# Half of batch 6's first product as seven half products a pair, u added by accumulating DMA in batches 5 and 6, and two tail units moved behind batch 6

## The chip, the cores and the metric

The kernel runs on one core of one Trainium2 chip. The metric is the device time of one execution in microseconds, lower is better. The core has five engines that run their own instruction streams in order and meet through semaphores: TensorE (PE in the profile, its weight loads PEld), VectorE (DVE), ScalarE (ACT), GpSimd (POOL) and SyncE (SP). DMA transfers are issued from the queues of SP, GpSimd and ScalarE.

## The reference

Eight batches of 576 tokens go through a linear attention with eight heads of 64, and then through a mixer with a low-rank product over the tokens and a two-layer product over the channels:

```
q_p, k_p = [relu(q)*cos, relu(q)*sin], [relu(k)*cos, relu(k)*sin]   # cos, sin of the position
kv = k_p^T v ;  z = sum of k_p over the tokens                      # per batch and head
x  = (q_p kv) / (q_p z + 1e-6)                                      # 576 x 512 per batch
u  = x + V^T (U^T x)                                                # rank 32, over the tokens
out = u + relu(u @ w_ch1) @ w_ch2                                   # 512 -> 2048 -> 512
```

Inputs and output are float32; the kernel computes the products in bf16.

## The kernel before, in words

**Tiling.** The 576 tokens of a batch are held as four chunks of 128 and a tail of 64. The tails of two batches share one tile of 128 rows, so there are four tail pairs (`pr`), the last of batches 6 and 7. `u_bf[b]` holds u of a batch, `uT[b]` its transpose, made by DMA transposes on SP's queue (`utr_dma`), two chunks each. `uT_tl[pr]` is the transpose of a tail pair.

**First product.** `g1_main(b, j)` computes one block of 128 of the 2048 hidden rows for 512 tokens: four 128x512 matmuls into a PSUM bank, then a relu on ScalarE into `hid[b]`. There are 16 blocks per batch. `g1_tail(pr, jq)` does four blocks for a tail pair with sixteen 128x128 matmuls.

In batch 7 the first product is done by Strassen-Winograd instead. Blocks p and p + 8 are a *pair*; rows, tokens and the inner dimension are each cut in two, and seven products of half size take the place of eight. `g1_cross(b, p, i)` is one of the seven (two 128x256 matmuls) and `g1_join(b, p, ...)` brings them together: P1, U2 and P5 are copies of PSUM into `kept` by ScalarE, C11, C12 and C22 additions by VectorE, with relus on both. The steps of a pair are named `opened` (products 1 and 2, P1, C11), `second` (6 and 5, U2, P5), `third` (7, C22) and `closed` (3 and 4, C12, relus, `max`). The products 3 to 7 need sums of weights (`w1_sum`, four, each in two halves of columns; half 1 serves pairs 4 to 7) and sums of quarters of u transposed (`uT_sum`, four a batch), which VectorE makes beforehand.

**Second product.** Batches 2 to 7 do it by the same scheme in `half_part(b, n, k, form)`: fourteen half parts of eight 128x256 matmuls a batch. It needs sums of `hid` (`hid_sum`, VectorE). The results go to float32 tiles `o_sb` (eight buffers), onto which u is added. In most batches VectorE adds u as it reads PSUM. In batches 5 and 6 (`LENT`) ScalarE copies PSUM, and GpSimd adds u in `half_store` with a 128x512 `tensor_tensor`, just before the store. Batch 5's stores go through GpSimd's queue, batch 6's through SP's.

**Order.** All is ordered by hand. `slots` is a list of units of TensorE work; `put(at, f)` hangs f behind slot number `at`. A unit's instructions and what hangs behind it go into each engine's stream in that order. In the slots of batch b's first product, half parts of batch b - 1 alternate with blocks of batch b: batch 5 starts at slot 156 and batch 6 at slot 190, with four tail units of pair 2 (slots 186 to 189) between them, batch 7 at slot 220. Behind the slots hangs the attention of a later batch (`attention_plan`): `q_prep`, `k_prep`, `v_prep`, the DMA transposes of q, `kv_unit`, five `x_unit`s, `A_unit` (U^T x), `u_mm` (V^T times that), four `u_add`s (VectorE, u = x + that) with the transposes of u between them, and `u_tail` for the tails of two batches. Its place is a number `w` per batch in `PLAN`; batch 7's is 191, so that its first `x_unit` stands at slot 195, the last at 203, `A_unit` at 205, `u_mm` at 207 and its last transposes of u at 212.

**PSUM.** There are eight banks: g0, g1, g2, T, o0, o1 and X, which is a pair of banks. In batches 3 to 6 blocks of the first product alternate between g0 and g1, half parts use o0 and o1, `x_unit` uses X. `A_unit` uses g2 (called "s"). `u_mm` and `u_tail` want four banks, one for each quarter of the rank-32 product: X's two, T and g2. A bank is free for its next use when the last reader of its content is done.

Of the kernel before, what the change touches and what calls it, by code (L numbers as in the profile page):

```python
# [17 lines left out]
def kernel(  # L18
# [446 lines left out]

    va = {}

    def u_mm(b, *spare):
        if b not in u_bf:
            u_bf[b] = pool.tile([P, 4, 4, P], BF16, tag="u_bf", bufs=3, name="u_bf")  # L470
        va[b] = four_banks(*spare)
        for c in range(4):
            for j in range(4):
# [11 lines left out]
            in1=va[b][j].rearrange("p (c n) -> p c n", c=4), op=ALU.add,  # L485
        )

    def u_tail(pr, *spare):
        u_tl[pr] = pool.tile(
            [P, DM], BF16, tag="k_p" if pr == 3 else "u_tl", bufs=1, name="u_tl"  # L490
        )
        vt = four_banks(*spare)
        for i in range(2):
            for j in range(4):
# [6 lines left out]
        for j in range(4):  # L501
# [8 lines left out]

    def uTt_alloc(pr):
        if pr not in uT_tl:
            uT_tl[pr] = pool.tile([P, 4, P], BF16, tag="uT_tl", bufs=1, name="uT_tl")

    def utr_dma(b, c0, c1):
        if c0 < 4:
# [113 lines left out]

    def uT_sum(b, i):

        if i == 1:
            t = pool.tile([P, 4, 2, 2, P], BF16, tag="vst", bufs=1, name="uT_s")
            for n in range(4):
                uT_s[b, n + 1] = t[:, n]
# [10 lines left out]
    def g1_cross(b, p, i):  # L647

        if (b, p) not in cross:
            if b not in hid:
                hid[b] = pool.tile([P, NJ, 512], BF16, tag="hid", bufs=2, name="hid")
            xy, z = [
                psum.tile([P, 512], FP32, tag=tag, bufs=1, name="c_ps") for tag in CROSS[p % 2]
            ]
            cross[b, p] = {"X": xy[:, 0:256], "Y": xy[:, 256:512], "Z": z[:, 0:256]}
        w = cross[b, p]
        cs = slice(p * P, p * P + P)
        to, lhs, rhs, first = {  # L660
            1: lambda: ("X", W1[0], uT_quarter(b, 0, 0), True),
            2: lambda: ("Y", W1[1], uT_quarter(b, 1, 0), False),
            3: lambda: ("Z", w1_s[4], uT_quarter(b, 1, 1), False),
            4: lambda: ("X", W1[3], uT_s[b, 4], False),
            5: lambda: ("Z", w1_s[1], uT_s[b, 1], True),
            6: lambda: ("X", w1_s[2], uT_s[b, 2], False),
            7: lambda: ("X", w1_s[3], uT_s[b, 3], False),
        }[i]()
        for d in range(2):
            nc.tensor.matmul(  # L670
                out=w[to].rearrange("p (c t) -> p c t", c=2), lhsT=lhs[:, d, cs],
                rhs=rhs[:, d], start=(first and d == 0), stop=(d == 1),
                skip_group_check=not first,
            )

    def g1_join(b, p, i):

        w, lo, hi = cross[b, p], slice(0, 256), slice(256, 512)
        top, low = hid[b][:, p, :], hid[b][:, p + 8, :]

        def relu(o, x):
            nc.scalar.activation(out=o, in_=x, func=AF.Relu, bias=0.0, scale=1.0)

        if i == "C11":
            diff(top[:, lo], w["P1"], w["Y"], ALU.add)
        elif i == "C22":
            diff(low[:, hi], w["P5"], w["X"], ALU.add)
            relu(low[:, hi], low[:, hi])
        elif i == "C12":
            diff(top[:, hi], w["U2"], w["Z"], ALU.add)  # L690
            relu(low[:, lo], w["X"])
            V_.tensor_scalar(out=top, in0=top, scalar1=0.0, scalar2=None, op0=ALU.max)
        else:
            if (b, "kept") not in cross:
                cross[b, "kept"] = pool.tile([P, 2, 3, 256], FP32, tag="q_pT", bufs=1, name="kept")
# [239 lines left out]
    def half_store(b, n, i):  # L935
        eng = nc.gpsimd if b < B - 2 else nc.sync
        c = n + 2 * i
        if b in LENT:
            o = halves[b, n]["o"][i]
            add(G_, by_n(o), by_n(o), u_bf[b][:, :, c, :])  # L940
        eng.dma_start(  # L941
            out=out[b].rearrange("(m k) n -> m k n", k=9)[:, c : c + 6 : 5, :],
            in_=halves[b, n]["o"][i],
        )
# [28 lines left out]
    def spare(at):  # L973
# [11 lines left out]
        4: (100, (-20, 1, V_, V_), (-13, 2, A_, V_), -12, (-9, -4, -4)),  # L985
        5: (127, (-24, 2, A_, A_), (-14, 2, A_, V_), (-14, -8, -5), (-8, -4, -4)),
        6: (157, (-23, 2, A_, A_), (-14, 2, A_, V_), (-14, -8, -6), (-8, -4, -4)),
        7: (191, (-24, 2, A_, A_), (-14, 2, A_, V_), (-14, -12, -10), ()),
    }

    def attention_plan(b):
# [42 lines left out]
        put(a_at, A_unit, tag=True)  # L1034
        odd = b % 2 == 1


        def two(at):
            return [T1, ("s", 1)] if at >= 88 else [spare(at)] * 2

        plan.append((w + a_at + 2, lambda: u_mm(b, *two(w + a_at + 2))))
        for j in range(4):
            put(a_at + 2 + j + (2 if b > 4 and j > 1 else 0), u_add, j)
        put(a_at + 3, utr_dma, 0, 2)
        put(a_at + (7 if b > 4 else 5), utr_dma, 2, 4)
        if odd:
            plan.append(
                (w + a_at + 9, lambda: u_tail(b // 2, *two(w + a_at + 9)))
            )
# [307 lines left out]
    for b in range(3, B - 1):  # L1357
# [10 lines left out]
        if b % 2:  # L1368
            tail_slots(b // 2)
        if b == 3:  # L1370
            tail_out(b // 2)

    at = len(slots)
# [7 lines left out]
    sums(b7 - 1, 0, (at, at + 1, at + 6))  # L1381
    sums(b7 - 1, 1, (at + 13, at + 15, at + 19))

    def opened(p):
        g1_cross(b7, p, 1)
        g1_cross(b7, p, 2)
        g1_join(b7, p, "P1")
        g1_join(b7, p, "C11")

    def second(p):  # L1390
        g1_cross(b7, p, 6)
        g1_cross(b7, p, 5)
        g1_join(b7, p, "U2")
        g1_join(b7, p, "P5")

    def third(p):
        g1_cross(b7, p, 7)
        g1_join(b7, p, "C22")

    def closed(p):  # L1400
        g1_cross(b7, p, 3)
        g1_cross(b7, p, 4)
        g1_join(b7, p, "C12")

    def group(p, first, then):
        def go():
            if p < 8:
                first(p)
            if p > 0:
                then(p - 1)  # L1410

        return go

    groups = [
        group(p, *fs) for p in range(9) for fs in ((opened, third), (second, closed))
    ]
    halfs = [(n, i7) for n in range(2) for i7 in range(7)]
# [8 lines left out]
    for i, go in enumerate(groups):  # L1426
        slots.append(go)
        if i < 14:
            n, i7 = halfs[i]
            slots.append(lambda n=n, i7=i7: half_part(b7 - 1, n, i7, "with g"))  # L1430
            if i7 > 4:
                put(len(slots), lambda n=n, i7=i7: half_store(b7 - 1, n, i7 - 5))
        else:
            slots.append(lambda j=i - 14: tail_cross(j))
    at = len(slots)
# [76 lines left out]
```

## Time and profile before

| | us |
|---|---|
| median of 3 runs | 295.01 (293.94 to 295.38) |
| the profiled execution | 294.26 |
| its span | 292.5 |
| mean granted clock of TensorE | 0.998 |

Stretches of the span and what the engines were busy in them (us):

| stretch | length | PE | DVE | ACT | POOL |
|---|---|---|---|---|---|
| 176.35 to 206.69: first product of batch 5, second of 4 | 30.34 | 30.08 | 20.68 | 19.24 | 5.44 |
| 206.69 to 210.41: four tail units of pair 2 | 3.72 | 3.72 | 3.58 | 2.89 | 0.62 |
| 210.41 to 225.90: batch 6, first half | 15.49 | 15.33 | 8.70 | 7.30 | 1.09 |
| 225.90 to 240.19: batch 6, second half | 14.29 | 14.19 | 10.87 | 6.11 | 4.45 |
| 240.19 to 269.95: first product of batch 7, second of 6 | 29.76 | 29.04 | 21.69 | 17.88 | 6.71 |
| 269.95 to 292.50: second product of 7 and the last tails | 22.55 | 18.50 | 13.77 | 3.67 | 5.21 |

How to read it: an engine whose busy time fills a stretch sets its length, and the others wait for it. Busy time alone does not show waits inside a stretch; for these the timeline gives each instruction with its start, its duration and, in brackets, the idle time before it and what ended that. "L576" is line 576 of the kernel. Names are those of the program: `g_ps` is PSUM of a whole block, `c_ps` of a half product of the first product, `h_ps` of a half part, `x_ps`, `a_ps`, `va_ps` of `x_unit`, `A_unit` and `u_mm` or `u_tail`, `gt_ps` of a tail unit.

### The profile page before, as it was taken

How to read it: one execution, taken by the hardware profiler on the slowest of the kernel's cores; microseconds unless marked ns; L12 is line 12 of the kernel's file. 1: busy time of each engine (PE TensorE's matmuls, PEld its weight loads, DVE VectorE, ACT ScalarE, POOL GpSimd, SP SyncE). 2: the span in 40 equal slices, each digit the busy share in tenths (PEclk: the TensorE clock that was granted, in tenths of full speed). 3: DMA queues.
4: the chain of work that ended last, by engine and by line, in shares of the span. 5: the costliest groups of instructions: out<-in, count | busy, mean ns of one | idle time of the engine just before them, and what ended most of it. 6: DMA issues, size and time to landing. Idle time of an engine off the chain costs nothing.

```text
span 292.5 us, 7212 instructions
## 1 busy us (share of the span) xinstructions
PE 284.3 (97%) x2884; PEld 191.8 (66%) x2920; DVE 203.6 (70%) x484; ACT 166.9 (57%) x340; POOL 55.8 (19%) x92
## 2 busy tenths in 40 slices
PE   8999999999999999999999999999999999999994
PEld 4675564447545446676767667766776667889883
DVE  5977855496875697556547793778827687865773
ACT  2955742276882767577736765298753445567210
POOL 6520500000020004202300501040202331302330
PEclk9999999999999999999999999999999999999999
DMA  7999999999998989998799939974800321101023
GB/s 226 304 254 251 275 160 222 205 318 228 340 194 175 294 212 259 240 315 237 147 250 265 242 88 280 231 266 92 215 0 4 110 68 59 50 24 72 2 94 125
DMA packets 90949, 54.07 MB, mean 185 GB/s; under 512 B 58564, under 2 KB 87620, under 8 KB 90916
## 3 DMA queue, kind: packets, MB, share of 16 engines
q1 hardware_dynamic: 84420, 43.94, 60.2%
q0 software_dynamic: 6304, 9.47, 14.6%
q8 instruction: 23, 0.38, 0.5%
q10 hardware_dynamic: 192, 0.20, 0.2%
q14 instruction: 10, 0.08, 0.1%
HBM read 36.86 MB, written 9.44 MB: 158 GB/s over the span
## 4 chain that ended last, share of the span: by engine, by line
PE 90%; DMA 3%; ACT 2%; DVE 2%; issue 1%; ACTq 0%; DVEq 0%
PE g_ps L576 31%; PE h_ps L882 26%; PE o_ps L750 11%; PE gt_ps L710 5%; PE c_ps L670 4%; PE kv_ps L347 3%; PE x_ps L422 3%; DMA qst<-in_q_dram 2%; DVE uT_s L608 1%; PE a_ps L445 1%; PE h_ps L750 1%; PE g_ps L593 1%; DMA uT<-u_bf 1%; PE va_ps L475 1%; PE t_ps L365 1%
## 5 line engine op out<-in xcount | busy, mean ns | idle before, releaser
L576 PE MATMUL g_ps<-uT,w_bf 128*128 128x512 bf16 x408 | 103.5, 379 | 1.3
L585 ACT ACTIVATE hid<-g_ps 128x512 bf16<-128x512 f32 x112 | 65.8, 599 | 64.2 <-PE g_ps L576 63.8
L576 PEld LDWEIGHTS <-w_bf 128*128 128x128 bf16 x434 | 40.9, 98 | 36.7
L882 PEld LDWEIGHTS <-hid 128*128 128x128 bf16 x480 | 45.4, 98 | 9.6
L882 PE MATMUL h_ps<-w_bf,hid 128*128 128x256 bf16 x288 | 37.1, 273 | 0.0
L750 PE MATMUL o_ps<-w_bf,hid 128*128 128x512 bf16 x122 | 29.4, 379 | 0.4 <-issue 0.2
L882 PE MATMUL h_ps<-w_s,S 128*128 128x256 bf16 x208 | 26.5, 273 | 0.0
L131 POOL CAST v_ext<-vst 128x512 bf16<-128x512 f32 (+1 forms) x23 | 15.2, 687 | 57.4 <-DMA vst<-in_v_dram 26.8
L838 DVE TENSOR_TENSOR o_sb<-o_sb,h_ps 128x256 f32<-128x256 f32 (+1 forms) x36 | 15.5, 433 | 15.1 <-PE h_ps L882 9.9
L882 PE MATMUL h_ps<-w_s,hid 128*128 128x256 bf16 x192 | 24.9, 273 | 0.0
L483 DVE TENSOR_TENSOR u_bf<-x_bf,va_ps 128x512 bf16<-128x512 bf16 x27 | 17.7, 680 | 8.3 <-PE va_ps L475 4.7
L838 POOL TENSOR_TENSOR o_sb<-o_sb,u_bf 128x512 f32<-128x512 f32 x10 | 12.1, 1205 | 57.5 <-DVE o_sb L838 43.8
L882 PEld LDWEIGHTS <-S 128*128 128x128 bf16 x208 | 19.9, 98 | 4.4
L838 DVE TENSOR_TENSOR o_sb<-u_bf,h_ps 128x256 f32<-128x256 bf16 x28 | 11.7, 417 | 14.3 <-PE h_ps L882 14.2
L941 POOL DMA_DIRECT2D out_dram<-o_sb x16 | 9.9, 619 | 54.0 <-DVE o_sb L838 51.2
L750 PEld LDWEIGHTS <-hid 128*128 128x128 bf16 x128 | 11.5, 98 | 12.2
L710 PE MATMUL gt_ps<-uT_tl,w_bf 128*128 128x128 bf16 x256 | 16.1, 219 | 0.0
L432 DVE TENSOR_TENSOR x_bf<-x_ps,rec 128x512 bf16<-128x512 f32 x22 | 15.2, 691 | 0.8
L710 PEld LDWEIGHTS <-w_bf 128*128 128x128 bf16 x256 | 14.9, 98 | 0.8
L306 ACT ACTIVATE k_p<-kst,cosw 128x512 bf16<-128x512 f32 x20 | 14.2, 713 | 0.1
L608 DVE TENSOR_TENSOR hid<-kept,c_ps 128x256 bf16<-128x256 f32 x24 | 9.4, 418 | 6.6 <-PE c_ps L670 3.5
L306 ACT ACTIVATE q_p<-qst,sinw 128x512 bf16<-128x512 f32 x18 | 12.6, 709 | 1.7 <-DMA qst<-in_q_dram 1.7
(188 smaller groups left out, 429.0 us busy)
## 6 DMA issues: line engine op xcount, KB each, us to landing
qst<-in_q_dram SPq DMA_DIRECT2D x14, 512.0 KB, 6.0
kst<-in_k_dram SPq DMA_DIRECT2D x14, 512.0 KB, 6.6
vst<-in_v_dram SPq DMA_DIRECT2D x12, 512.0 KB, 6.8
out_dram<-o_sb POOLq DMA_DIRECT2D x19, 256.0 KB, 3.7
out_dram<-o_sb SPq DMA_DIRECT2D x16, 256.0 KB, 2.5
w_bf<-in_moe_w_ch_dram POOLq DMA_DIRECT2D x7, 512.0 KB, 13.7
qst<-in_q_dram SPq DMA_DIRECT2D x2, 640.0 KB, 13.1
kst<-in_k_dram SPq DMA_DIRECT2D x2, 640.0 KB, 7.1
```

The lines of the kernel that those rows point to most:

```text
L131: eng.tensor_copy(out=o, in_=i)
L306: nc.scalar.activation(out=o, in_=i, func=AF.Relu, bias=0.0, scale=w)
L432: nc.vector.tensor_tensor(out=x_of(b, c, rows).rearrange("p (g i d) -> p g i d", g=2, d=D), in0=view[:, :, :, 0:D], in1=rec[rows].unsqueez ...
L483: nc.vector.tensor_tensor(out=u_bf[b][:, j, :, :], in0=x_bf[b][:, :, ns], in1=va[b][j].rearrange("p (c n) -> p c n", c=4), op=ALU.add,)
L576: nc.tensor.matmul(out=g_ps.rearrange("p (c t) -> p c t", c=4), lhsT=w1_bf[:, d, j * P : j * P + P], rhs=uT[b][:, d, :, :], start=(d == 0) ...
L585: nc.scalar.activation(out=hid[b][:, j, :], in_=g_ps, func=AF.Relu, bias=0.0, scale=1.0)
L608: V_.tensor_tensor(out=o, in0=x, in1=y, op=op)
L670: nc.tensor.matmul(out=w[to].rearrange("p (c t) -> p c t", c=2), lhsT=lhs[:, d, cs], rhs=rhs[:, d], start=(first and d == 0), stop=(d == 1 ...
L710: nc.tensor.matmul(out=g_ps[:, jj, :], lhsT=w1_bf[:, d, j * P : j * P + P], rhs=uT_tl[pr][:, d, :], start=(d == 0), stop=(d == 3),)
L750: nc.tensor.matmul(out=o[:, cols], lhsT=lhs[:, j, c * P : c * P + P], rhs=w2_bf[:, j, cols], start=(j == 0), stop=(j == NJ - 1),)
L838: eng.tensor_tensor(out=o, in0=x, in1=y, op=ALU.add)
L882: nc.tensor.matmul(out=acc, lhsT=lhs[:, j, :], rhs=rhs[:, j, :], start=(j == 0 and at is not None), stop=(j == 7), skip_group_check=at is ...
```

## The change

- **Batch 6's first product.** Pairs 0 to 2 and block 3 (with block 11, its partner) stay whole products. Pairs 4 to 7 become half products. Product 5 with its copy P5 is taken from `second` and done a step later (`sixth`, then `fifth` beside the next pair's `opened`): in turn a slot does `opened` of a pair with `fifth` and `third` of the pair before, and the next slot `closed` of the pair before with `sixth` of the pair. X and Y of a pair lie in g0 or g1, Z of every pair in T. The sums of weights are made earlier (slots 180 to 187 and, for the halves of columns that batch 7 alone needs, 199 and 211), four sums of u of batch 6 are new, and `kept` of batch 6 takes the buffer of q_p.
- **T is no longer free for the attention of batch 7**, so that `A_unit` uses g2 and its copy goes to ScalarE, and `u_mm` and `u_tail` do three quarters in X and g2 first, and the fourth, two slots or one slot later, in X again.
- **Adding u in batches 5 and 6.** GpSimd's `tensor_tensor` becomes an accumulating DMA from GpSimd's queue, which reads bf16 `u_bf` and adds it to float32 `o_sb`. The store waits for it. The last two accumulations and stores of batch 5 come eight and nine slots later.
- **Order.** Two of the four tail units of pair 2 go behind batch 6: batch 6 starts at slot 188, the two units and the last `closed` are slots 218 to 220, and batch 7 starts at 221. Batch 7's attention has w = 189 in place of 191. `uT_tl` of the last pair takes x_bf's buffer.

```diff
-    def u_mm(b, *spare):
+    def u_mm(b, *spare, js=range(4)):
...
-        va[b] = four_banks(*spare)
+        va.setdefault(b, {}).update(zip(js, four_banks(*spare)))
...
-            xy, z = [
-                psum.tile([P, 512], FP32, tag=tag, bufs=1, name="c_ps") for tag in CROSS[p % 2]
-            ]
-            cross[b, p] = {"X": xy[:, 0:256], "Y": xy[:, 256:512], "Z": z[:, 0:256]}
+            of_x, of_z = CROSS[p % 2] if b == B - 1 else (("g0", "g1")[p % 2], "T")
+            xy = psum.tile([P, 512], FP32, tag=of_x, bufs=1, name="c_ps")
+            cross[b, p] = {"X": xy[:, 0:256], "Y": xy[:, 256:512], "of_z": of_z}
         w = cross[b, p]
+        if i == 5:
+            z = psum.tile([P, 512], FP32, tag=w["of_z"], bufs=1, name="c_ps")
+            w["Z"] = z[:, 0:256]
...
         if b in LENT:
             o = halves[b, n]["o"][i]
-            add(G_, by_n(o), by_n(o), u_bf[b][:, :, c, :])
+            nc.gpsimd.dma_start(out=by_n(o), in_=u_bf[b][:, :, c, :], accum_op=ALU.add)
...
-        7: (191, (-24, 2, A_, A_), (-14, 2, A_, V_), (-14, -12, -10), ()),
+        7: (189, (-24, 2, A_, A_), (-14, 2, A_, V_), (-12, -10, -8), ()),
...
-        plan.append((w + a_at + 2, lambda: u_mm(b, *two(w + a_at + 2))))
+        if b == B - 1:
+            plan.append((w + a_at + 2, lambda: u_mm(b, ("s", 1), js=(0, 1, 2))))
+            plan.append((w + a_at + 4, lambda: u_mm(b, js=(3,))))
+        else:
+            plan.append((w + a_at + 2, lambda: u_mm(b, *two(w + a_at + 2))))
...
+                plan.append((w + a_at + 9, lambda: u_tail(b // 2, ("s", 1), js=(0, 1, 2))))
+                plan.append((w + a_at + 10, lambda: u_tail(b // 2, js=(3,))))
...
+    def beside_g(b, m):
+        n, i7 = halfs[m]
+        slots.append(lambda: half_part(b, n, i7, "with g"))
+        if i7 > 4:
+            later = {5: 8, 6: 9}[i7] if (b, n) == (b6 - 1, 1) else 0
+            put(len(slots) + later, lambda: half_store(b, n, i7 - 5))
 
     at = len(slots)
-    b7 = B - 1
+    sums(b6 - 1, 0, (at, at + 1, at + 3))
+    sums(b6 - 1, 1, (at + 13, at + 15, at + 19))
     for i, half, sl in (
-        (1, 0, -4), (1, 1, -3), (3, 0, -3), (3, 1, -2), (2, 0, -1), (2, 1, 21), (4, 0, 22), (4, 1, 25),
+        (1, 1, -8), (2, 1, -6), (3, 1, -4), (1, 0, -3), (4, 1, -2), (3, 0, -1), (2, 0, 11), (4, 0, 23),
     ):
-        put(at - 30 + sl, lambda i=i, half=half: w1_sum(i, half))
+        put(at + sl, lambda i=i, half=half: w1_sum(i, half))
+    for i in range(4):
+        put(at + 1 + i, lambda i=i: uT_sum(b6, i + 1))
+    units = [g1(b6, j) for p in range(3) for j in (p, p + 8)] + [g1(b6, 3)]
+    units.append(lambda: [g1_main(b6, 11), opened(b6, 4)])
+    units.append(crossed((sixth, b6, 4)))
+    for p in range(5, 8):
+        units.append(crossed((opened, b6, p), (fifth, b6, p - 1), (third, b6, p - 1)))
+        units.append(crossed((closed, b6, p - 1), (sixth, b6, p)))
+    units.append(crossed((fifth, b6, 7), (third, b6, 7)))
+    slots += units[0:2]
+    for m in range(14):
+        beside_g(b6 - 1, m)
+        slots.append(units[2 + m])
...
+    slots.append(lambda: tail_late(2))
+    slots.append(crossed((closed, b6, 7)))
+    slots.append(lambda: tail_late(3))
```

Here `tail_late(j)` is `g1_tail(2, j)` into X (j = 2) or g2 (j = 3).

More of the change, by code (lines that the diff above doesn't have):

```diff
@@ L486, in u_add, with u_tail @@
         )
[L488 to L492, printed above, removed]
+    def u_tail(pr, *spare, js=range(4)):
+        if pr not in u_tl:
+            u_tl[pr] = pool.tile(
+                [P, DM], BF16, tag="k_p" if pr == 3 else "u_tl", bufs=1, name="u_tl"
+            )
+        vt = dict(zip(js, four_banks(*spare)))
         for i in range(2):
-            for j in range(4):
+            for j in js:
                 rows = slice(j * R, j * R + R)
@@ L500, in u_tail @@
                 )
-        for j in range(4):
+        for j in js:
             ns = slice(j * P, j * P + P)
@@ L512, in uTt_alloc @@
         if pr not in uT_tl:
[L513 removed]
+            uT_tl[pr] = pool.tile(
+                [P, 4, P], BF16, tag="x_bf" if pr == 3 else "uT_tl", bufs=1, name="uT_tl"
+            )
     def utr_dma(b, c0, c1):
@@ L1356 @@
     alone = len(slots)
-    for b in range(3, B - 1):
+    for b in range(3, B - 2):
         at = len(slots)
@@ L1367, with opened, second @@
                 slots.append(g1(b, 2 + 7 * n + i7))
-        if b % 2:
+        if b == 3:
             tail_slots(b // 2)
-        if b == 3:
             tail_out(b // 2)
+        elif b % 2:
+            slots.extend(lambda pr=b // 2, j=j: g1_tail(pr, j) for j in range(2))
+    b6, b7 = B - 2, B - 1
+    def opened(b, p):
+        g1_cross(b, p, 1)
+        g1_cross(b, p, 2)
+        g1_join(b, p, "P1")
+        g1_join(b, p, "C11")
+    def second(b, p):
+        g1_cross(b, p, 6)
+        g1_cross(b, p, 5)
+        g1_join(b, p, "U2")
+        g1_join(b, p, "P5")
@@ new lines, in sixth, with fifth, third, closed @@
+    def sixth(b, p):
+        g1_cross(b, p, 6)
+        g1_join(b, p, "U2")
+    def fifth(b, p):
+        g1_cross(b, p, 5)
+        g1_join(b, p, "P5")
+    def third(b, p):
+        g1_cross(b, p, 7)
+        g1_join(b, p, "C22")
+    def closed(b, p):
+        g1_cross(b, p, 3)
+        g1_cross(b, p, 4)
+        g1_join(b, p, "C12")
+    def crossed(*steps):
+        def go():
+            for f, b, p in steps:
+                f(b, p)
+        return go
+    halfs = [(n, i7) for n in range(2) for i7 in range(7)]
@@ L1379 @@
+    slots.append(lambda: tail_late(3))
+    at = len(slots)
     for i in range(4):
         put(at - 4 + i, lambda i=i: uT_sum(b7, i + 1))
[L1381 to L1403, printed above, removed]
-    def group(p, first, then):
[L1406 to L1412, printed above, removed]
+    sums(b6, 0, (at, at + 1, at + 6))
+    sums(b6, 1, (at + 13, at + 15, at + 19))
+    def group(p, first, then):
+        return crossed(*([(first, b7, p)] if p < 8 else []), *([(then, b7, p - 1)] if p else []))
@@ L1428 @@
         if i < 14:
[L1429 to L1432, printed above, removed]
+            beside_g(b6, i)
         else:
```

32 lines of the change are left out of this document (22 added, 10 removed).

## The prediction

> **What bounds the kernel now.** I read the page first (busy shares, then the chain that ended last), then the stretches by stage, then every engine's timeline from 200 us on.
>
> ```profile
> PE 284.3 (97%) x2884; PEld 191.8 (66%) x2920; DVE 203.6 (70%) x484; ACT 166.9 (57%) x340; POOL 55.8 (19%) x92
> ...
> PE 90%; DMA 3%; ACT 2%; DVE 2%; issue 1%; ACTq 0%; DVEq 0%
> ```
>
> TensorE is the bound: 97% busy, 90% of the last chain. So time moves by TensorE work taken out, or by TensorE waits made or removed. The rows say what a matmul costs in a stream (columns: start, us, engine, line, operation, count; a row's us includes the drain of its last matmul, so prices come from starts):
>
> ```profile
> 223.94 1.03 PE L576 MATMUL g_ps<-uT,w_bf 128*128 128x512 bf16 x4
> 224.80 0.42 PE L422 MATMUL x_ps<-kv,q_pT 128*128 128x65 bf16 x8
> 225.06 1.03 PE L882 MATMUL h_ps<-w_s,hid 128*128 128x256 bf16 x8
> 225.93 1.03 PE L576 MATMUL g_ps<-uT,w_bf 128*128 128x512 bf16 x4
> 226.89 0.24 PE L445 MATMUL a_ps<-x_tl,U_bf 128*32 128x128 bf16 x4
> ...
> 227.28 1.05 PE L882 MATMUL h_ps<-w_bf,hid 128*128 128x256 bf16 x8
> ```
>
> Four 512-wide matmuls take 0.866 us (223.94 to 224.80), 0.2165 each; eight 256-wide ones 0.87 (225.06 to 225.93), 0.109 each; `x_unit` takes 0.26, and a switch to the 32-row matmuls of `A_unit` or `u_mm` 0.09 besides. From 206.69 to 240.19 TensorE hardly waits. At the start of batch 7's first product it does:
>
> ```profile
> 240.62 1.04 PE L882 MATMUL h_ps<-w_bf,hid 128*128 128x256 bf16 x8
> 242.35 0.60 PE L670 MATMUL c_ps<-uT_s,w_s 128*128 128x256 bf16 x4 [0.69 <-DVE hid L608]
> ```
>
> Eight matmuls from 240.62 end at 241.49, so it stands until 242.35: 0.86 us. VectorE and GpSimd say why:
>
> ```profile
> 238.13 0.42 DVE L608 TENSOR_TENSOR uT_s<-uT 128x512 bf16<-128x512 bf16 x1
> 238.58 1.26 DVE L608 TENSOR_TENSOR uT_s<-uT,uT_s 128x512 bf16<-128x512 bf16 x1
> 239.76 0.41 DVE L608 TENSOR_TENSOR uT_s<-uT 128x512 bf16<-128x512 bf16 x1
> 240.10 1.87 DVE L608 TENSOR_TENSOR uT_s<-uT,uT_s 128x512 bf16<-128x512 bf16 x1
> ```
> ```profile
> 238.30 1.26 POOL L838 TENSOR_TENSOR o_sb<-o_sb,u_bf 128x512 f32<-128x512 f32 x1 [8.93 <-DVE o_sb L838]
> 239.86 0.63 POOL L941 DMA_DIRECT2D out_dram<-o_sb  x1 [0.30 <-POOL o_sb L838]
> 240.50 1.17 POOL L838 TENSOR_TENSOR o_sb<-o_sb,u_bf 128x512 f32<-128x512 f32 x1
> ```
>
> Two sums took 1.26 and 1.87 us where their like took 0.41; each ended 0.3 us after a GpSimd addition ended (239.56, 241.67). Those two additions held VectorE for 2.3 us, and this makes the 0.86.
>
> **The change, part by part.**
>
> *TensorE work.* A pair of row blocks of batch 6 costs 8 x 0.2165 = 1.732 as whole products and 14 x 0.109 = 1.526 as half products: 0.206 saved, four pairs 0.82 us, all on the path. Splitting `u_mm` and `u_tail` adds no matmul but two switches, +0.18. The two tail units (16 matmuls in 0.93) only move.
>
> *The stall at 241.49.* The additions become accumulating DMAs, and the attention of batch 7 starts two slots earlier before a product that starts one later. In the count below the last addition to u ends at 234.3, its transpose lands 2.73 later ("DMA uT<-u_bf" of the chain, 235.25 to 237.98), at 237.05; the four sums then stand behind joins of batch 6 and end at 241.85, 1.0 before TensorE wants them (242.84). So -0.86. The additions that hold VectorE at 251 to 265 go too: `max` at L692 took 1.08 and 0.69 beside them and 0.29 elsewhere, mostly in VectorE's own slack: -0.1.
>
> *New TensorE waits.* Here the change can lose. I step the engines through the changed order with durations from the rows: VectorE starts the next instruction 0.33 after a 256-wide join or addition (0.42 row), 0.6 after a 512-wide one (0.69); ScalarE starts 0.20 after TensorE moves on; a copy of 256 is 0.38, a relu frees ScalarE after 0.49. Batch 6 starts at 206.69 + 2 x 0.93 = 208.55 on the clock of before.
>
> (a) `A_unit`, slot 203. Its last four matmuls need the last `x_unit` (slot 201, x ready 223.8). In slot 201 `opened` now puts the join C11 and a sum of batch 5 ahead of it on VectorE. C11 waits for ScalarE's copy P1, behind the relu of block 11: relu 223.14, P1 223.63 to 224.01. So C11 224.05, sum 224.4, reciprocal and product 225.0 to 226.1 (1.12 in the rows of before). TensorE arrives at 225.1: **+1.0**. Before, two whole slots lay between these; now one is a quarter of its size.
>
> (b) The fourth part of `u_mm`, slot 207. It reuses bank pair X, free only when `u_add` 0 and 1 are done. VectorE: C11 of pair 5 at 228.0 (after P1), C22 of pair 4, `u_add` 0 at 228.7, an output addition at 229.4, `u_add` 1 to 230.42. TensorE arrives at 229.95: **+0.5**. Queued behind it are the next half parts, nothing else can run.
>
> (c) The fourth part of `u_tail`, slot 213, the same bank. VectorE is busy without a gap from 229.4: hidden sums, C12 and `max` of pairs 4 and 5, `u_add` 2 and 3 to 234.3, C12, a weight sum, an addition, two tail additions to 236.33. TensorE arrives at 235.85: **+0.5**.
>
> Batch 7 then starts at 241.5 (240.19 before) and finds no stall at its second step.
>
> *Covered work.* The sums of weights move to slots 180 to 187: six of 0.69, on a VectorE that waited 0.92 twice for TensorE between 203 and 206 and was to idle 4.21 us after 212; the sums of batch 6's u, 4 x 0.42, go into that idle time. Were it gone, the first cost would be (a) again. ScalarE swaps two relus of 0.60 per pair for 3 x 0.38 + 0.42 + 0.39 = 1.95: +0.75 in about 3.4 us, where it waited 0.5 per slot for TensorE. The transposes of u move with batch 7's attention; SP's queue has only stores behind them.
>
> *The accumulating DMA* is nowhere in the trace. Landing: nearest row is GpSimd's store of the same 256 KB, 3.7 us in the median; the bounds are 2.5 (SP's store) and 13.7 (its weight load). GpSimd waits that out before the store in batch 5, SP in batch 6; nothing on the path reads `o_sb` before its buffer returns. What the *issue* does to VectorE is open: the sum at 240.10 began during the issue at 239.86 to 240.49 and got nothing done before the addition took over, the sum at 239.76 was not touched. So 0 to 0.62 per issue that meets a two-input SBUF sum. With 3.7 to land, GpSimd issues at 223.0, 227.2, 227.8 and 232.0; only the last meets one (the hidden sum at 231.7), and (c) would grow by up to 0.6. I take 0, as the row at 239.76 has the clean overlap, and keep 0.6 for the range.
>
> The Trainium skill ("SBUF — State Buffer", Who interferes with whom) says that a VectorE instruction with two SBUF inputs contends with a GpSimd instruction that reads SBUF, not with one that only writes, and infers that issuing descriptors doesn't stop `tensor_tensor`. The additions agree (1.26 and 1.87 against 0.41). By it the sum is mine with 0 here; by the row at 240.10 it would be 0.6 more.
>
> **Sum:** -0.82 + 0.18 - 0.86 - 0.1 + 1.0 + 0.5 + 0.5 = **+0.4 us**. The profiled execution took 294.26 (span 292.5 and 1.8 around it), 0.75 under the median 295.01 of runs from 293.94 to 295.38. Put on the median: **295.4 us**, 0.1% over. Runs of one kernel spread by 0.5%, about what a measurement can tell from no change.
>
> **Rivals.**
> 1. *The three waits don't stand* (VectorE gets ahead, the copies come sooner): 295.01 - 0.82 + 0.18 - 0.86 - 0.1 = 293.4. For it: VectorE idles about 1.1 us before C11 of pair 4 and 1.3 before C11 of pair 5. Against: that idling is the wait for P1, and it comes ahead of the work that TensorE needs.
> 2. *GpSimd's issues hold VectorE* (slower). Place: the second half of batch 6 and batch 7's first product, where two-input sums lie between joins. Batches 5 and 6 issue eight accumulations and four stores in this stretch. With the 0.62 on (c) and two more in batch 7: +0.4 + 1.9, 297.3. It decides from two issues that reach the path. For it: the row at 240.10. Against: the row at 239.76, and 8 us of VectorE idling in batch 7's stretch (21.7 busy of 29.76).
> 3. *The stall at batch 7 stays*: the 1.0 us of margin is eaten by a later transpose or later joins. +0.86, 296.3.
> 4. *An output buffer returns late.* `o_sb` has eight; the last set reuses batch 6's second half, written from about 283, whose last accumulation starts near 266. It decides from 17 us for accumulation and store, against 3.7 + 2.5 by the rows. Then one wait of 2 us or more: 297.4.
>
> **How the numbers follow.** Forecast 0.42 (294.5 to 296.4), rival 1 0.27, rival 2 0.20, rival 3 0.08, rival 4 0.03. Faster by over 0.5% means below 293.53: most of rival 1, 0.22. Slower means above 296.49: rivals 2 and 4 and the edges of the forecast and of 3, 0.28. Within: 0.50. Range 293.2 (rival 1 with its spread) to 297.1 (most of rival 2).
>
> **What would show it.** Right: 56 half-product matmuls at about 0.109 in batch 6; gaps on TensorE before the last four `a_ps` matmuls (released by VectorE's `x_bf`), before the last `va_ps` ones of `u_mm` and of `u_tail`; batch 7's `uT_s` sums at 0.41 each; no stall at its second step. Wrong: no such gaps (rival 1), or `hid` and `S` sums of over 1 us beside POOL rows of DMA issue (rival 2), or c_ps matmuls of batch 7 waiting for `uT_s` (3), or for DMA on an `o_sb` write after 280 (4). What would make me wrong most easily is the order on VectorE around slot 201: if P1 is copied 1 us sooner, (a) is gone.

## The result and the profile after

The changed kernel takes 296.68 us in the median (296.26 to 297.74), the kernel before 295.19 (293.94 to 295.39) over the same number of runs: a ratio of 1.0064, 95% interval 1.0035 to 1.0092. It is slower by 0.6%, 1.3 us more than the 295.4 forecast and inside the range. Its profiled execution took 296.26, with a span of 294.5 against 292.5.

Busy time and the chain of waits, from the page of after:

```profile
PE 284.8 (97%) x2910; PEld 194.6 (66%) x2944; DVE 207.5 (70%) x503; ACT 169.3 (57%) x353; POOL 57.8 (20%) x92
...
PE 94%; DVE 3%; issue 1%; ACT 0%; DVEq 0%
```

TensorE was 90% of the last chain and is 94%; it is busy 0.5 us longer, not 0.64 shorter as 0.82 off and 0.18 on would make it. Where the time went is seen when the span is cut at four events that every kernel here has: the first tail unit of pair 2, the first half product of batch 7, the second product of batch 7 alone, the end. The cuts are starts of rows on TensorE's timeline (us; the first column holds the same TensorE instructions in every kernel, and varies by 2.1 us over the profiled executions of all but the two padded ones; a stretch is far steadier, 33.50 us in before and 33.51 in e1 below, 35.81 in after and in e2, pairs with the same TensorE work in it):

| kernel | to the tail unit | to batch 7 | to the lone product | to the end |
|---|---|---|---|---|
| before | 206.69 | 33.50 | 29.76 | 22.5 |
| after | 206.93 | 35.81 | 29.11 | 22.6 |
| after less before | +0.24 | **+2.31** | **-0.65** | +0.1 |

The stretch that holds batch 6 was reckoned at +1.36 (-0.82 + 0.18 + 1.0 + 0.5 + 0.5), the next at -0.96. Both came out on the bad side. TensorE's timeline of after shows the three waits that were forecast, each where it was placed (columns as before: start, us, engine, line, operation, count, and in brackets the idle time before it and what ended that):

```profile
223.86 1.04 PE L891 MATMUL h_ps<-w_s,hid 128*128 128x256 bf16 x8
225.02 0.38 PE L676 MATMUL c_ps<-uT_s,w_s 128*128 128x256 bf16 x2
...
226.66 0.24 PE L445 MATMUL a_ps<-x_bf,U_bf 128*32 128x128 bf16 x4 [0.93 <-DVE x_bf L432]
...
231.18 0.39 PE L475 MATMUL va_ps<-A_sb,V_bf 32*128 32x128 bf16 x4 [0.46 <-DVE u_bf L483]
...
237.49 0.24 PE L497 MATMUL va_ps<-A_sb,V_tl 32*64 32x128 bf16 x2 [0.50 <-DVE u_tl L504]
...
243.17 1.04 PE L891 MATMUL h_ps<-w_bf,hid 128*128 128x256 bf16 x8
244.31 0.60 PE L676 MATMUL c_ps<-uT_s,w_s 128*128 128x256 bf16 x4
```

They are 0.93, 0.46 and 0.50, in sum 1.89 against 2.0 forecast. VectorE's timeline of after gives the reason for the first of them, and for two gaps that no bracket shows:

```profile
222.68 0.41 DVE L847 TENSOR_TENSOR o_sb<-o_sb,h_ps 128x256 f32<-128x256 f32 x1
224.55 0.42 DVE L611 TENSOR_TENSOR hid<-kept,c_ps 128x256 bf16<-128x256 f32 x1 [1.46 <-ACT kept L129]
224.88 0.69 DVE L833 TENSOR_TENSOR S<-hid 128x1024 bf16<-128x1024 bf16 x1
...
225.92 0.69 DVE L432 TENSOR_TENSOR x_bf<-x_ps,rec 128x512 bf16<-128x512 f32 x1
...
243.84 0.42 DVE L611 TENSOR_TENSOR hid<-kept,c_ps 128x256 bf16<-128x256 f32 x1 [0.33 <-ACT kept L129]
244.18 0.69 DVE L833 TENSOR_TENSOR S<-hid 128x1024 bf16<-128x1024 bf16 x1
244.90 0.69 DVE L833 TENSOR_TENSOR S<-S,hid 128x1024 bf16<-128x1024 bf16 x1
```

VectorE stands 1.46 us for the copy P1 (`kept`) with the last `x_unit`'s work queued behind C11. The same C11 ends at 224.97, and the sixth product of the pair, which goes into the bank that C11 reads (X and Y are its halves), starts at 225.02. By the prediction's price of 0.109 the eight matmuls from 223.86 end at 224.73, so that is a gap of 0.29. The second gap is at batch 7's second step: the eight from 243.17 end at 244.04, C11 ends at 244.26 and TensorE starts at 244.31, 0.27 after it could. The stall of 0.86 did not go to nothing.

GpSimd's timeline of after, with the accumulating DMA:

```profile
227.93 1.32 POOL L949 DMA_DIRECT2D o_sb<-u_bf  x1
231.91 0.63 POOL L950 DMA_DIRECT2D out_dram<-o_sb  x1 [2.65 <-DMA o_sb<-u_bf]
...
244.02 1.32 POOL L949 DMA_DIRECT2D o_sb<-u_bf  x1
```

The sums `S` at 244.18 and 244.90 run beside the issue of 244.02 to 245.34 and take 0.69 each, their usual time. One `max` beside an issue, at 265.62, takes 0.48 in place of 0.29.

### The profile page after: what moved, and what is told of

The parts are those of the page before. It is cut to its first block, busy times and chain, and to the rows that moved or that the text cites. A ratio compares the mean times of both kernels' runs of the same rounds, so it can differ in the third digit from the quotient of the medians.

```text
span 294.5 us, 7310 instructions
## 1 busy us (share of the span) xinstructions
PE 284.8 (97%) x2910; PEld 194.6 (66%) x2944; DVE 207.5 (70%) x503; ACT 169.3 (57%) x353; POOL 57.8 (20%) x92
## 3 DMA queue, kind: packets, MB, share of 16 engines
q1 hardware_dynamic: 84420, 43.94, 59.7%
## 4 chain that ended last, share of the span: by engine, by line
PE 94%; DVE 3%; issue 1%; ACT 0%; DVEq 0%
PE g_ps L579 29%; PE h_ps L891 26%; PE o_ps L759 10%; PE c_ps L676 6%; PE gt_ps L719 5%; PE kv_ps L347 3%; PE w_ps L234 3%; PE x_ps L422 3%; PE h_ps L759 1%; PE a_ps L445 1%; PE g_ps L596 1%; PE va_ps L475 1%; PE t_ps L365 1%; PE t_ps L377 1%; PE z_ps L1236 1%
## 5 line engine op out<-in xcount | busy, mean ns | idle before, releaser
L579 PE MATMUL g_ps<-uT,w_bf 128*128 128x512 bf16 x378 | 95.5, 380 | 1.1
L588 ACT ACTIVATE hid<-g_ps 128x512 bf16<-128x512 f32 x104 | 61.0, 598 | 57.1 <-PE g_ps L579 56.3
L579 PEld LDWEIGHTS <-w_bf 128*128 128x128 bf16 x402 | 37.8, 98 | 34.7 <-issue 0.2
L611 DVE TENSOR_TENSOR hid<-kept,c_ps 128x256 bf16<-128x256 f32 x36 | 14.2, 418 | 12.5 <-ACT kept L129 9.1
L949 POOL DMA_DIRECT2D o_sb<-u_bf x8 | 10.4, 1295 | 36.6 <-DVE o_sb L847 35.5
L719 PEld LDWEIGHTS <-w_bf 128*128 128x128 bf16 x256 | 15.1, 98 | 0.7
L129 ACT ACTIVATE kept<-c_ps 128x256 f32<-128x256 f32 x36 | 12.5, 380 | 4.9 <-PE c_ps L676 4.1
```

What stands on the lines that cost most here:

```text
L579: nc.tensor.matmul(out=g_ps.rearrange("p (c t) -> p c t", c=4), lhsT=w1_bf[:, d, j * P : j * P + P], rhs=uT[b][:, d, :, :], start=(d == 0) ...
L588: nc.scalar.activation(out=hid[b][:, j, :], in_=g_ps, func=AF.Relu, bias=0.0, scale=1.0)
L611: V_.tensor_tensor(out=o, in0=x, in1=y, op=op)
L719: nc.tensor.matmul(out=g_ps[:, jj, :], lhsT=w1_bf[:, d, j * P : j * P + P], rhs=uT_tl[pr][:, d, :], start=(d == 0), stop=(d == 3),)
```

## The experiments

Each timed ratio is to the kernel before on the same chip, whose median was 294.87, 294.85 and 294.87 in the three sets. Stretches are those of the table, each from one profiled execution; where no other is named, it is the one from the tail unit to batch 7, which holds batch 6.

### What the split of u_mm and u_tail costs by itself

`e3_whole_split` is after with whole products in all of batch 6; `e4_whole_unsplit` puts `u_mm` and `u_tail` back into one piece as well, and the copy of `A_unit` back on VectorE. (`A_unit` is one unit and lies in g2 in every kernel here; of it the change moved only the copy.) Both keep the accumulating DMA, the moved tail units and the attention at 189.

```diff
-    units = [g1(b6, j) for p in range(3) for j in (p, p + 8)] + [g1(b6, 3)]
-    units.append(lambda: [g1_main(b6, 11), opened(b6, 4)])
...
+    units = [g1(b6, j) for p in range(8) for j in (p, p + 8)]
...
-    slots.append(crossed((closed, b6, 7)))
+    slots.append(lambda: None)
```
and for e4 besides
```diff
-            put(a_at, A_unit, "s", 1, A_)
...
+        put(a_at, A_unit, tag=True)
...
-            plan.append((w + a_at + 2, lambda: u_mm(b, ("s", 1), js=(0, 1, 2))))
-            plan.append((w + a_at + 4, lambda: u_mm(b, js=(3,))))
...
+        plan.append((w + a_at + 2, lambda: u_mm(b, *two(w + a_at + 2))))
...
-                plan.append((w + a_at + 9, lambda: u_tail(b // 2, ("s", 1), js=(0, 1, 2))))
-                plan.append((w + a_at + 10, lambda: u_tail(b // 2, js=(3,))))
...
+            plan.append((w + a_at + 9, lambda: u_tail(b // 2, *two(w + a_at + 9))))
```

> The changed kernel with batch 6 in whole products again; u_mm and u_tail are still split, two tail units still lie behind batch 6. TensorE work +0.82. My theory: the wait before a_ps (0.93) and the wait of product 6 for C11 (0.29) are gone with the joins, of the two waits for bank X about half remains, and so does the cost of the extra small groups of matmuls (0.5): 0.6 to 1.0 below the changed kernel, 295.7 to 296.1. Rival (the split of u_mm and u_tail costs nothing of itself, all is the half products): 294.5 or less. Rival (half products are not to blame): 297.5.

> As the run before, and u_mm, u_tail and A_unit as in the kernel before (T is free for them); what is left of the change is the accumulating DMA, the two tail units behind batch 6 and the attention of batch 7 at 189. My theory: no waits but the 0.27 at the second step of batch 7, work as in the kernel before: 294.5, as the first run of this call. Rival (moving the tail units costs, by a wait for a bank or by later first sums of batch 6's hidden rows): over 295.2.

e3: 295.60 us, 1.0026 [1.0011, 1.0040], stretch 34.41. e4: 295.23, 1.0018 [1.0004, 1.0031], stretch 33.35. So the split costs 1.06 us without any half product, and what e4 keeps of the change costs this stretch nothing: e4's is 0.15 below that of before. The fourth part of `u_mm` waits for `u_add` as in after (TensorE's timeline of e3):

```profile
230.40 0.39 PE L475 MATMUL va_ps<-A_sb,V_bf 32*128 32x128 bf16 x4 [0.31 <-DVE u_bf L483]
230.72 1.05 PE L891 MATMUL h_ps<-w_s,S 128*128 128x256 bf16 x8
```

The wait is 0.31 us; the rest is what a piece takes. TensorE's rows of before and then of after, each group of `u_mm` or `u_tail` with the start of the unit behind it:

```profile
229.12 0.40 PE L475 MATMUL va_ps<-A_sb,V_bf 32*128 32x128 bf16 x16
229.46 1.05 PE L882 MATMUL h_ps<-w_bf,hid 128*128 128x256 bf16 x8
...
235.65 0.26 PE L496 MATMUL va_ps<-A_sb,V_tl 32*64 32x128 bf16 x8
235.84 1.04 PE L576 MATMUL g_ps<-uT,w_bf 128*128 128x512 bf16 x4
```
```profile
228.69 0.40 PE L475 MATMUL va_ps<-A_sb,V_bf 32*128 32x128 bf16 x12
229.02 1.05 PE L891 MATMUL h_ps<-w_bf,hid 128*128 128x256 bf16 x8
...
231.50 1.05 PE L891 MATMUL h_ps<-w_s,S 128*128 128x256 bf16 x8
...
237.66 1.05 PE L891 MATMUL h_ps<-w_bf,hid 128*128 128x256 bf16 x8
```

From start to start, the sixteen matmuls of `u_mm` take 0.34 us, the twelve of its three quarters 0.33 and the four of its fourth quarter, from 231.18, 0.32. For `u_tail` it is 0.19 for eight and, from 237.49, 0.17 for two. The trace's starts of single matmuls say why. The four quarters of `u_mm` lie in four strips of 32 rows, and the matmuls of one chunk of tokens, one to a strip, start 0.003 to 0.005 apart, the next chunk 0.05 to 0.07 later. A quarter alone has one matmul in each such step and needs as many steps. The eight of `u_tail` all start within 0.03. So a piece costs nearly as much as the whole, with 0.09 or more in front of it. Against before, this and the same at `A_unit`, which its wait cuts in two (0.17 from 226.66 to 226.84 for the last four), come to 0.99 us in after without the waits: about 0.5 at `u_mm`, 0.3 at `u_tail` and 0.2 at `A_unit`. In e3 it is 0.5 and 0.25 with `A_unit` whole, which with the wait of 0.31 is all but 0.02 of the 1.06.

e3 came out 0.1 under the 295.7 to 296.1 expected. e4's time stands 0.7 over the 294.5 expected; its end took 23.6 us, which e1 below takes up.

### Taking the three waits away

`e5_early` moves batch 7's attention one slot ahead, so that the last `x_unit` no longer shares a slot with the first `opened`; `e6_late_quarter` moves the fourth parts of `u_mm` and `u_tail` two slots back; `e7_both` does both.

```diff
-        7: (189, (-24, 2, A_, A_), (-14, 2, A_, V_), (-12, -10, -8), ()),
+        7: (188, (-23, 2, A_, A_), (-13, 2, A_, V_), (-11, -9, -7), ()),
```
```diff
-            plan.append((w + a_at + 4, lambda: u_mm(b, js=(3,))))
+            plan.append((w + a_at + 6, lambda: u_mm(b, js=(3,))))
...
-                plan.append((w + a_at + 10, lambda: u_tail(b // 2, js=(3,))))
+                plan.append((w + a_at + 12, lambda: u_tail(b // 2, js=(3,))))
...
-            put(a_at + 10, utr_dma, 4, 5)
+            put(a_at + (12 if b == B - 1 else 10), utr_dma, 4, 5)
```

> The changed kernel with the attention of batch 7 one slot earlier (188), its loads' uses and transposes of q where they were. Then the last x_unit stands a slot before opened of pair 4, and its chain on VectorE comes ahead of C11. My theory: the wait before a_ps (0.93 and its switch) is gone and product 6 of pair 4 no longer waits for C11 (0.29), the two waits for bank X stay: the stretch from the first tail unit of pair 2 to batch 7 is 34.5 us in place of 35.81, and the time 1.3 below the changed kernel, 295.4. Rival (VectorE is simply full in this stretch, and the waits move to the next place that needs it): the stretch stays within 0.4 us of 35.81.

> The changed kernel with the fourth quarters of u_mm and u_tail two slots later each, so that bank X is free when they come. My theory: the waits of 0.46 and 0.50 go, the one before a_ps and the cost of the small groups (0.6) stay: stretch 34.85, time 1.0 below the changed kernel, 295.7. Rival (VectorE is full): within 0.4 us of 35.81, with the wait at the same two instructions in their new place.

> Both edits together. My theory: the three waits are gone and the work saved by the half products shows: stretch 33.4 to 33.7, against 33.50 of the kernel before and 35.81 of the changed one, and batch 7's product 29.1: 2.2 below the changed kernel, 294.5, 0.6 below the kernel before. Rival (VectorE is full): 35 or more, 296 or more.

e5: 295.49 us, 1.0017 [1.0000, 1.0034], stretch 34.75. e6: 296.05, 1.0048 [1.0030, 1.0067], stretch 35.05. e7: 294.64, 0.9993 [0.9979, 1.0006], stretch 33.92. One slot is worth 1.06 us of the stretch and the two later quarters 0.76; both together 1.89. TensorE's timeline of e5 and then of e7:

```profile
225.69 0.40 PE L445 MATMUL a_ps<-x_bf,U_bf 128*32 128x128 bf16 x16
...
230.06 0.39 PE L475 MATMUL va_ps<-A_sb,V_bf 32*128 32x128 bf16 x4 [0.55 <-DVE u_bf L483]
...
236.10 0.24 PE L497 MATMUL va_ps<-A_sb,V_tl 32*64 32x128 bf16 x2 [0.43 <-DVE u_tl L504]
```
```profile
217.57 0.42 PE L422 MATMUL x_ps<-kv,q_pT 128*128 128x65 bf16 x8 [0.17 <-DVE x_tl L432]
...
231.42 0.39 PE L475 MATMUL va_ps<-A_sb,V_bf 32*128 32x128 bf16 x4
...
237.47 0.24 PE L497 MATMUL va_ps<-A_sb,V_tl 32*64 32x128 bf16 x2
```

In e5 the sixteen matmuls of `A_unit` on `x_bf` are one row and of the three waits only the other two are left; in e7 all three are gone. In both the gap of 0.29 goes too, as `A_unit` stands between C11 and the sixth product, and an `x_unit` comes too early for VectorE (the bracket of 0.17; by the prices it starts 0.33 late). That 1.89 is also the sum of the three waits in after is therefore chance: e7 saves the gap and the second piece of `A_unit` besides, and loses about as much at that `x_unit` and at a half product that starts 0.24 late.

e7 can't be told from the kernel before, and its stretch missed the 33.4 to 33.7 expected: it is 0.42 longer than before's, although it has 0.82 less of matmuls. The extra pieces of `u_mm` and `u_tail` take 0.8 of that, the `x_unit` 0.33 and the half product 0.24.

### Fewer half products

`e8_two_pairs` is after with half products in pairs 6 and 7 alone. `e11_two_pairs_whole_u` has `A_unit` and `u_mm` in one piece besides, and the fourth part of `u_tail` late; `e12_two_pairs_unsplit_early` has `u_tail` in one piece too and the attention a slot earlier.

```diff
-    units = [g1(b6, j) for p in range(3) for j in (p, p + 8)] + [g1(b6, 3)]
-    units.append(lambda: [g1_main(b6, 11), opened(b6, 4)])
-    units.append(crossed((sixth, b6, 4)))
-    for p in range(5, 8):
+    units = [g1(b6, j) for p in range(5) for j in (p, p + 8)] + [g1(b6, 5)]
+    units.append(lambda: [g1_main(b6, 13), opened(b6, 6)])
+    units.append(crossed((sixth, b6, 6)))
+    for p in range(7, 8):
```

> The kernel after with half products only in pairs 6 and 7; the split of u_mm and u_tail stays. If wait (a) comes from the join C11 of pair 4 in slot 201 (my step), it is gone, since no pair opens there: stretch (first tail unit of pair 2 to batch 7's first product) = 34.41 of the kernel with whole products and the split, less two pairs x 0.206, = 34.0 to 34.3, and the time 295.2 to 295.4. If a half-product pair costs more than it saves through its small groups (0.25 us each time, as the trace of after shows), the stretch stays at 34.4 or more.

> Half products in pairs 6 and 7 alone, A_unit and u_mm in one piece as before, u_tail's fourth quarter two slots later. If the split of u_mm costs what the whole products show (33.35 us of stretch unsplit against 34.41 split), the stretch is 33.35 - 0.41 + 0.35 for the split u_tail = 33.2 to 33.4 and the stall at batch 7 stays small: 294.0 to 294.3. By the rival (small groups eat what a pair saves) 33.8 and 294.6.

> As the last, but u_tail in one piece too, and batch 7's attention one slot earlier. Pair 6's third product then waits for the bank that u_tail's additions leave: if that is short, stretch 33.35 - 0.41 + 0.1 = 33.0 and 293.9; if the bank comes late, a wait of 0.5 to 1 us on TensorE before the first half product into that bank, and 294.4 to 294.9.

e8: 295.91 us, 1.0026 [1.0002, 1.0049], stretch 34.53. Wait (a) is gone with `opened` of pair 4, at the unchanged place of the attention: together with e5 this shows that C11 in that slot made it. But two pairs of half products won nothing against the whole products of e3 (34.41), where 0.41 was reckoned. e11: 294.91, 1.0004 [0.9982, 1.0026], stretch 33.58, against 33.35 of e4. e12: 294.42, 0.9990 [0.9967, 1.0013], stretch 33.82; its first guess of 33.0 missed. e11 was expected at 294.0 to 294.3 and came out above. VectorE and TensorE of e11 show one thing that eats the gain:

```profile
231.90 0.68 DVE L833 TENSOR_TENSOR hid<-hid 128x1024 bf16<-128x1024 bf16 x1
233.81 0.42 DVE L611 TENSOR_TENSOR hid<-kept,c_ps 128x256 bf16<-128x256 f32 x1 [1.23 <-ACT kept L129]
```
```profile
233.14 1.04 PE L891 MATMUL h_ps<-w_s,S 128*128 128x256 bf16 x8
234.29 0.38 PE L676 MATMUL c_ps<-uT_s,w_s 128*128 128x256 bf16 x2
```

Eight matmuls from 233.14 end at 234.01; C11 ends at 234.23, and the sixth product starts at 234.29, 0.28 late. The first pair of half products has one half part between `opened` and the product that goes into C11's bank, and copy, join and start don't fit under it. It is the gap of 225.02 in after, and that of batch 7's second step in every kernel without GpSimd's additions.

The rows name most of the rest of the lost 0.41, by the same prices. e8 has this gap with 0.27, 0.15 more than e3 in front of the last part of `u_tail`, and 0.07 before an `x_unit`. e11 has, besides the 0.28, the second piece of `u_tail` with 0.25 and 0.06 before an `x_unit`. In e12 the gap is 0.27, an `x_unit` starts 0.34 late, and 0.28 is lost in `u_tail`: its matmuls into g2 start at 233.53, when `u_add` 3, which reads g2 and stands behind C11 on VectorE, ends at 233.48. That leaves 0.05 or less of each difference.

e7, e11 and e12 can't be told from the kernel before, so none of them is shown to be faster than it.

### GpSimd's additions back

`e2_add_back` is after with GpSimd's `tensor_tensor` in place of the accumulating DMA.

```diff
-            nc.gpsimd.dma_start(out=by_n(o), in_=u_bf[b][:, :, c, :], accum_op=ALU.add)
+            add(G_, by_n(o), by_n(o), u_bf[b][:, :, c, :])
```

> The changed kernel with the accumulating DMA undone (GpSimd adds u again). My theory: the waits of TensorE in the second half of batch 6 have nothing to do with it, so the three gaps before a_ps, va_ps of u_mm and va_ps of u_tail stay (0.9, 0.5, 0.5 us) and the time is that of the changed kernel within 0.6 us, rather above (an addition may hold a sum again): 296.7 to 297.3. Rival (the DMA costs): 0.5 us or more below the changed kernel, under 296.2.

297.39 us, 1.0094 [1.0070, 1.0118]. The stretch with batch 6 is 35.81, as in after; the next is 29.78, as in before (29.76), with a stall of 0.94 at batch 7's second step. The time is 0.1 us above the 296.7 to 297.3 expected. Its VectorE and GpSimd at that step:

```profile
241.42 1.03 DVE L698 TENSOR_SCALAR hid<-hid 128x512 bf16<-128x512 bf16 x1
...
242.85 0.42 DVE L611 TENSOR_TENSOR hid<-kept,c_ps 128x256 bf16<-128x256 f32 x1 [0.41 <-ACT kept L129]
243.19 1.50 DVE L611 TENSOR_TENSOR uT_s<-uT 128x512 bf16<-128x512 bf16 x1
```
```profile
241.14 1.15 POOL L847 TENSOR_TENSOR o_sb<-o_sb,u_bf 128x512 f32<-128x512 f32 x1 [11.76 <-DVE o_sb L847]
...
243.23 1.17 POOL L847 TENSOR_TENSOR o_sb<-o_sb,u_bf 128x512 f32<-128x512 f32 x1
```

The sum at 243.19 takes 1.50 and ends 0.29 after the addition of 243.23; in after its like takes 0.42. So the DMA, not the attention's earlier place, took the hold away, and its issue costs the stretch ahead nothing.

### The accumulating DMA alone, and two pads

`e1_dma_alone` is the kernel before with that one line as a DMA. `e9_dma_pad` and `e10_late_pad` are e1 with a new one-column tile among the constants and twelve memsets of it on VectorE, at the start or in batch 7's first product.

```diff
+    pad = const.tile([P, 1], FP32)
+    for _ in range(12):
+        V_.memset(pad, 0.0)
```
and in e10 the same tile with the memsets as
```diff
+    for sl in (8, 10, 12, 14):
+        put(len(slots) + sl, lambda: [V_.memset(pad, 0.0) for _ in range(3)])
```

> The kernel before with one part of the change: u is added by accumulating DMA in batches 5 and 6. My theory: the DMA is harmless and takes the two GpSimd additions off VectorE, so the two long sums of u (1.26 and 1.87 us) become 0.41 each and the stall at the second step of batch 7 falls from 0.86 to about 0.27 (the rest is the wait for join C11): 0.6 to 0.7 us faster than before, 294.5. Rival (the accumulating DMA is what made the changed kernel slow, by its issue of 1.3 us on GpSimd or its late landing): slower than before by 0.5 us or more.

> The kernel before with the accumulating DMA alone, and twelve more VectorE memsets of one column in the first microseconds, where VectorE waits for the first load. In the run with the DMA alone batch 7's product came out 0.59 us shorter, but the end, from the start of the last second product on, 0.93 longer (23.48 against 22.55); there 8 KB of instructions were fetched at 290.71, beside the last store, whose completion SP saw 1.3 us later. VectorE has 578 instructions there, and also in the other kernel with a long end (576, 577, 600 and 602 in those without). My theory: the fetch belongs to VectorE's code, and with twelve more instructions it comes some 10 us sooner and the end is 22.6 again: 294.3, 0.6 below the kernel before. Rival (the long end belongs to the accumulating DMA or is chance): the end stays at 23.4, 295.4, or the fetch stays at its place.

> The kernel before with the accumulating DMA alone, and 12 memsets of one column on VectorE in batch 7's first product (0.7 us of VectorE, which idles 8 us there). The accumulating DMA alone had an end of 23.5 us, with an instruction fetch beside the last store, against 22.6 of before. If the place of that fetch makes the 0.9 us, the pad moves it, the end is 22.5 to 22.7 and the time 0.6 to 0.9 lower than that of the accumulating DMA alone (295.49): 294.6 to 294.9. If not, 295.5. Nothing ahead of 240 us changes in the program, so the loads of batches 3 to 5 should not be moved, as they were by the pad at the start (296.91).

e1: 295.49 us, 1.0015 [1.0000, 1.0029], not the gain expected. Its stretches are 33.51 and 29.17: the 0.59 of batch 7 is there, with the attention where it was. In its profiled execution the end took it away: 23.5 us against 22.5. In e1 and e4 alone, of all these kernels, an 8 KB fetch of instructions lies beside the last store, at 290.71 and 290.11, and the last store of 128 KB lands later. The DMA view of the window from 288 to 292 us, of before and then of e1 (for a transfer: operation, count, size, median us from issue to landing; the fetch is the row of q14, with packets, MB and share of time):

```profile
out_dram<-o_sb ACTq DMA_DIRECT2D x1, 128.0 KB, 1.8
```
```profile
q14 instruction: 1, 0.01, 0.6%
...
out_dram<-o_sb ACTq DMA_DIRECT2D x1, 128.0 KB, 2.8
```

In e9 and e10 this fetch comes at 289.30 and 286.41, 3.2 and 5.3 us ahead of the last store's issue, that store lands in 1.8 and the end takes 22.5 in both. This part of the expectation held, in one profiled execution each; the times did not. e9 took 296.91 (1.0076 [1.0058, 1.0093]) and e10 298.46 (1.0109 [1.0076, 1.0143]). Both lose their time long before: batch 7's stretches are e1's, but the first column of the table is 210.86 and 210.07 against 207.54, and the rows of TensorE's waits of e10 up to 145 us, which e1 hasn't, are these, 0.98 of the 2.5 us:

```profile
67.17 3.61 PE L577 MATMUL g_ps<-uT,w_bf 128*128 128x512 bf16 x16 [0.38 <-ACT hid L586]
86.22 0.41 PE L476 MATMUL va_ps<-A_sb,V_bf 32*128 32x128 bf16 x16 [0.23 <-DVE A_sb L131]
89.89 0.25 PE L348 MATMUL kv_ps<-v_ext,k_p 128*128 128x65 bf16 x3 [0.37 <-POOL v_ext L131]
```

e10 runs no other instruction than e1 before 240 us. What differs there is the new tile among the constants, which can move the tiles made after it; the traces don't hold their addresses. The DMA views of e1 and then of e10:

```profile
q1 hardware_dynamic: 84420, 43.94, 61.0%
...
uT<-u_bf SPq DMA_TRANSPOSE x14, 2.8
```
```profile
q1 hardware_dynamic: 84420, 43.94, 64.8%
...
uT<-u_bf SPq DMA_TRANSPOSE x14, 3.6
```

The same packets take more time, and e9's, with 66.1% and 3.5, do too; the unpadded kernels have 59.7 to 61.2% and 2.8 to 3.1. So the slower DMAs go with the new tile. That they do so because tiles moved, and that the lost time comes from them, is argued and not shown: no run had a pad of another size.

## Why the prediction was right and wrong

- **Work, -0.82.** The half products are there (`c_ps` matmuls at 0.109 each), so the term stands as TensorE time; but two pairs, reckoned at -0.41, won nothing on the path (e8 against e3 +0.12; e11 against e4 +0.23, of which 0.25 is the split `u_tail`). The term left out what a first pair costs: the sixth product starts 0.28 late behind C11.
- **"two switches, +0.18".** This is the step that failed most. The prediction took a split to add "no matmul but two switches" of 0.09. A piece of `u_mm` or `u_tail` takes as long as the whole (0.32 against 0.34, 0.17 against 0.19), since the matmuls of a whole run side by side; and `A_unit`, cut in two by its wait, pays again. Measured: +0.99.
- **(a) +1.0, (b) +0.5, (c) +0.5.** 0.93, 0.46, 0.50, in the places and for the reasons given: e5 and e8 take (a) away, each with C11 out of that slot, e6 takes (b) and (c) away with time for the bank, and e7 all three.
- **The stall at 241.49, -0.86.** The four sums take 0.42 each as forecast and are in time (the last ends at 243.52). But C11 is next in the chain: 0.27 of the stall stays in every kernel without the hold, and 0.59 is won. So the held sums did not make all of the 0.86 in before, as the prediction read it. The prediction asked what is late next for the sums alone. The -0.1 for the additions at 251 to 265 can't be told apart from it: the stretch is 0.65 shorter, 0.59 in e1.
- **Accumulating DMA, issue at 0.** Right, with the wrong size of issue: 1.3 us, not 0.62. The Trainium skill ("SBUF — State Buffer", Who interferes with whom) infers that `tensor_tensor` takes only the read interface of the port pair that VectorE and GpSimd share, and the generation of descriptors the write interface; the sums of 0.69 beside an issue agree. Landing is 3.6 us, against 3.7 taken from the store.
- **Rivals.** 1 (no waits) fell with the three brackets, 2 (issues hold VectorE) with e2 and the sums (one `max` of 0.48 aside), 4 (`o_sb` late) with an end of 22.6. 3 came in part: 0.27 of 0.86.

In sum, the stretch with batch 6: -0.82 + 1.89 + 0.99 + 0.29 = +2.35 (2.31 measured). The three waits were right in place and size. The price of the split was wrong in kind and not only in size, and the wait for C11 was missed twice, in batch 6 (0.29) and in batch 7 (0.27). The time fell outside the likeliest case (294.5 to 296.4) by 0.3 us. It lies inside the range because that went up to 297.1 for rival 2, which did not happen, so that much is luck.

## What to carry to other kernels

Before splitting a small unit, look in its rows at what a part of it takes from start to start: where its matmuls run side by side, a part can take as long as the whole. Here the extra pieces cost 1 us where the work saved was 0.8. When a wait is taken off the path, step the chain to the next thing that TensorE needs, since a join that was hidden under the old wait ends up as the new one. And before a difference of half a per cent is put down to an edit, compare stretches that hold the same instructions: the first stretch alone varied by 2.1 us here, and an end by 1 us beside an instruction fetch.

## What was not expected of the hardware

- Four matmuls of 32 rows in one strip of the array took 0.32 us to the next unit, sixteen in four strips 0.34 (after, 231.18; before, 229.12).
- A one-column tile among the constants went with a kernel 1.4 us (e9) and 3.0 us (e10) slower than e1 by the medians, with the packets of the SP queue at 66.1% and 64.8% of 16 engines' span in place of 61.0%, and transposes of u at 3.5 and 3.6 us in place of 2.8. The cause is open.
- An 8 KB instruction fetch beside the last store went with a landing of 2.8 and 2.9 us in place of 1.8 and an end 1 us longer (e1, e4).
- An accumulating DMA of 256 KB, bf16 onto float32 in SBUF, holds GpSimd 1.3 us to issue (0.63 for a plain store of as many bytes) and lands in 3.6 us.
- Beside such an issue a VectorE `max` took 0.48 in place of 0.29 (after, 265.62), and beside a GpSimd addition 1.03 (e2, 241.42).
